# Spectral weights loaded into buffers that attention has finished with, and x put in channel order before its product

## The chip, the cores and the metric

The kernel runs on one core of one Trainium2 chip. The metric is the device time of one execution, in microseconds (us), median of several. A run is called slow when it is over 1.5% above the fastest of the same kernel; only fast runs are compared. The times of single instructions come from the profile of one execution; its span is about 1.8 us shorter than the reported time. In it PE is the engine of the matrix products, DVE, ACT and POOL are the vector, scalar and general engines, and L115 is line 115 of the kernel. POOL also issues the loads, which the DMA engines carry from HBM into SBUF, the memory on the chip; "the queue" is the stream of these loads.

## The reference, cut to what matters

```python
# attention: q, k, v [8, 8, 576, 64], causal window of 64
scores = where(mask, q @ k.T / 8, -1e9);  attn = softmax(scores);  x = attn @ v   # x: [8, 576, 512]
# spectral mix: 64 modes, each with a real and an imaginary 512 x 512 matrix
X = rfft(x, axis=1)[:, :64]
Y = X @ (w_r + 1j * w_i)            # one complex matrix for each mode
y = irfft(Y, n=576, axis=1)
u = x + y
out = u + relu(u @ w_ch)            # w_ch: 512 x 512, "the channel matrix"
```

There are 128 weight matrices (w_r and w_i of 64 modes). Each is 1 MB in HBM as float32 (1.049 million bytes) and becomes 0.524 million bytes in SBUF as bfloat16. They are most of the data that the kernel moves.

## The kernel before: the parts that matter

Attention runs first, in 36 windows of 512 columns. While it runs, POOL issues loads for the first 18 weights, as many as there are buffers (5 in `wlate`, 13 in `wearly`). Then come the modes, each with the two products of its weights. From mode 10 on, one "channel" tile is mixed in after each mode: x times the channel matrix, kept as Z0. The time ends with a tail that turns the spectrum back and writes the result.

```python
    LW, EW = 5, 13
    wlate  = ... tile_pool(name="wlate", bufs=LW)                  # kept through the modes
    wearly = p1 ... tile_pool(name="wearly", bufs=EW, side="right")  # p1: freed after attention
    acons  = p1 ...   # kT, vt of even and odd batches, masks
    rawp   = p1 ... bufs=2       # raw k, q, v of a batch (rk, rq, rv)
    ...
    small  = p1 ... bufs=2       # rcp: reciprocals of the row sums
    ...
    def load_w(i, pool, tag):
        m, im = divmod(i, 2)
        wt = pool.tile([128, NC, DM], BF16, name="wt", tag=tag)
        nc.gpsimd.dma_start(out=wt, in_=src[m].rearrange("(p c) e -> p c e", c=NC))
        wtiles[i] = wt
    ...                                                    # attention, 36 windows
    early(EARLY);  p1.close()
    Z0  = late.tile([128, len(tiles), DM], FP32R, name="Z0")       # over the attention buffers
    wcx = late.tile([128, NC, DM], FP32R, name="wcx", tag="wch")
    nc.gpsimd.dma_start(out=wcx, in_=moe_w_ch.rearrange("(p c) e -> p c e", p=128))

    def mode(m):
        for i in (2 * m, 2 * m + 1):
            if i >= nw:
                load_w(i, wlate, "wl")     # waits until mode has freed one of the five buffers
        ...                                # 32 products psy <- XQ, wt

    def channel(i):
        ... transposes of x_sb[:n, bb, tt, c, :] into pst;  xT = copy of pst
        ... psz = xT @ wcx;  nc.scalar.copy(out=Z0[:, i, :], in_=psz)
        xc = xtp.tile(...)                 # then put x in channel order for the tail
        nc.scalar.copy(out=xc[:n], in_=x_sb[:n, bb, tt, :, :])
        nc.vector.tensor_copy(out=view(x_sb[:n], ...), in_=view(xc[:n], ...))

    for m in range(10 + len(tiles)):
        mode(m)
        if m >= 10: channel(m - 10)
    ...
    wch = late.tile(..., tag="wch")        # the channel matrix again, rows in another order
    nc.gpsimd.dma_start(out=wch, in_=moe_w_ch.rearrange("(c p) e -> p c e", p=128))
    ...                                    # last modes, spectrum, tail
```

PE's order inside attention is fixed by the program (but for a few transposes of the channel stage that stand before its last weighing). On the other engines, and after attention, the compiler's scheduler orders the instructions by their data and their memory. And a tile placed over memory that another tile used waits until that tile is no longer used.

The softmax here doesn't subtract the row's maximum and nothing guards it: scores larger than these inputs give would overflow.

Of the kernel before, what the change touches and what calls it, by code (L numbers as in the profile page):

```python
# [10 lines left out]
FP32R = mybir.dt.float32r  # L11
BF16 = mybir.dt.bfloat16
# [8 lines left out]
def view(ap, off, dims):  # L21

    return bass.AP(ap.tensor, ap.offset + off, [list(ap.ap[0])] + [list(d) for d in dims])
# [3 lines left out]
def kernel(  # L27
# [10 lines left out]
    nc = tc.nc  # L38
    B, H, S, D = q.shape
    NM = moe_w_r.shape[0]  # L40
    DM = moe_w_ch.shape[0]
# [32 lines left out]

    p1 = ExitStack()
    wearly = p1.enter_context(tc.tile_pool(name="wearly", bufs=EW, side="right"))
    acons = p1.enter_context(tc.tile_pool(name="acons", bufs=1, side="right"))
    rawp = p1.enter_context(tc.tile_pool(name="rawp", bufs=2, side="right"))
    qtp = p1.enter_context(tc.tile_pool(name="qtp", bufs=2, side="right"))
    etp = p1.enter_context(tc.tile_pool(name="etp", bufs=4, side="right"))  # L80
    small = p1.enter_context(tc.tile_pool(name="small", bufs=2, side="right"))
# [26 lines left out]

    wtiles = {}

    def load_w(i, pool, tag):
        m, im = divmod(i, 2)
        wt = pool.tile([128, NC, DM], BF16, name="wt", tag=tag)
        src = moe_w_i if im else moe_w_r
        nc.gpsimd.dma_start(out=wt, in_=src[m].rearrange("(p c) e -> p c e", c=NC))  # L115
        wtiles[i] = wt
# [63 lines left out]

    load(1)

    kTs = [acons.tile([128, 4, S], BF16, name=f"kT{i}") for i in range(2)]

    vts = [acons.tile([128, 2, 4, 9, 4, 17], BF16, name=f"vt{i}") for i in range(2)]
    for vt in vts:
        nc.vector.memset(vt[:, 0, :, :, :, 16:17], 1.0)
    pso = ps_o.tile([128, 2, 512], FP32, name="pso")
# [133 lines left out]
    def early(n):  # L322
        nonlocal nw
        for _ in range(n):
            if nw < EARLY:
                load_w(nw, wlate if nw < LW else wearly, "wl" if nw < LW else "we")
                nw += 1

    def warm_up(n):
        for _ in range(n):  # L330
            nc.tensor.matmul(out=pss[2], lhsT=warm[:, 0:128], rhs=warm, start=True, stop=True)
# [3 lines left out]
    with tc.manual_schedule(engines={mybir.EngineType.PE}):  # L335
        warm_up(14)
        first = transpose_units(0)
        for i, j in enumerate((1, 2, 4, 5, 7, 8, 0, 3, 6, 9)):
            first[j]()
            if i in (2, 5):  # L340
                warm_up(6)
            if i in (6, 7, 8):
                warm_up(3)
        load(2)
        early(2)
        NU = 10
        sched = {}

        for b in range(1, B):
            start = -(-9 * (b - 1) // 2)  # L350
            for j in range(NU):
                sched.setdefault(start + j // 3, []).append((b, j))
        units = {}
        mask(0, 1)

        def unit(b, j):
            if b not in units:
                units[b] = transpose_units(b)
            units[b][j]()
            if j == NU - 1:  # L360
                if b + 2 < B:
                    load(b + 2)
                early(3)

        for w in range(NWIN + 1):
            todo = [lambda b=b: dft(b) for b in dfts]
            dfts.clear()
            todo += [lambda b=b, j=j: unit(b, j) for b, j in sched.get(w, [])]
            n = len(todo)
            if w < NWIN:  # L370
                scores(w)
            if w:
                cut = closes(w - 1)
                weigh(w - 1, 8 * w - 8, cut)
            if todo:
                todo.pop(0)()
            if w + 1 < NWIN:
                mask(w + 1, max(1, 3 - n))
            if todo:
                todo.pop(0)()  # L380
            if w:
                weigh(w - 1, cut, 8 * w)
            while todo:
                todo.pop(0)()
        while dfts:
            dft(dfts.pop(0))
        early(EARLY)
# [11 lines left out]
        tiles += [(b + i, t) for i in range(2) for t in range(NT - 1)] + [(b, NT - 1)]  # L399
    p2 = ctx.enter_context(ExitStack())  # L400
    late = p2.enter_context(tc.tile_pool(name="late", bufs=1, side="right", reuse_waits="tile"))
    Z0 = late.tile([128, len(tiles), DM], FP32R, name="Z0")

    trigI = late.tile([128, S + 128], FP32R, name="trigI")

    wcx = late.tile([128, NC, DM], FP32R, name="wcx", tag="wch")
    nc.gpsimd.dma_start(out=wcx, in_=moe_w_ch.rearrange("(p c) e -> p c e", p=128))
    YT = late.tile([128, NC, B, E0], FP32R, name="YT")
    YTl = late.tile([128, NC, 128], FP32R, name="YTl")

    ps_a = p2.enter_context(tc.tile_pool(name="ps_a", bufs=1, space=PSUM, reuse_waits="tile"))
    p2b = ExitStack()
    ps_y = p2b.enter_context(tc.tile_pool(name="ps_y", bufs=2, space=PSUM, reuse_waits="tile"))
    psy = None

    def mode(m):
        nonlocal psy
        for i in (2 * m, 2 * m + 1):
            if i >= nw:
                load_w(i, wlate, "wl")  # L420
        wr, wi = wtiles.pop(2 * m), wtiles.pop(2 * m + 1)
        if m % MG == 0:
            psy = ps_y.tile([128, MG, NC, 2 * B], FP32, name="psy")
        for e in range(NC):
            ee = slice(128 * e, 128 * e + 128)
            for c in range(NC):
                nc.tensor.matmul(out=psy[:, m % MG, e, :], lhsT=wr[:, c, ee],  # L427
                                 rhs=XQ[:, c, :, 1:3, m], start=(c == 0), stop=False)
            for c in range(NC):
                nc.tensor.matmul(out=psy[:, m % MG, e, :], lhsT=wi[:, c, ee],  # L430
                                 rhs=XQ[:, c, :, 0:2, m], start=False, stop=(c == NC - 1))
        if m == NM - 1:
            nc.vector.tensor_copy(
                out=view(YTl, 0, [[128, NC], [MG, 2 * B], [1, MG]]),
                in_=view(psy, 0, [[2 * B, NC], [1, 2 * B], [NC * 2 * B, MG]]))
        elif m % MG == MG - 1:
            for ri in range(2):
                evac(view(YT, m // MG * 2 * MG + ri * MG, [[B * E0, NC], [E0, B], [1, MG]]),
                     view(psy, ri, [[2 * B, NC], [2, B], [NC * 2 * B, MG]]), ri)

    with ExitStack() as p2a:
        ps_t = p2a.enter_context(tc.tile_pool(name="ps_t", bufs=2, space=PSUM, reuse_waits="tile"))
        ps_z = p2a.enter_context(tc.tile_pool(name="ps_z", bufs=2, space=PSUM, reuse_waits="tile"))
        xtp = p2a.enter_context(tc.tile_pool(name="xtp", bufs=2, side="right", reuse_waits="tile"))

        def channel(i):
            b, t = tiles[i]
            pst = ps_t.tile([128, NC, 128], BF16, name="pxt")
            parts = [(b, t, 0, 128)] if t < NT - 1 else [(b, t, 0, 64), (b + 1, t, 64, 64)]
            for bb, tt, r0, n in parts:  # L450
                for c in range(NC):
                    nc.tensor.transpose(out=pst[:, c, r0:r0 + n], in_=x_sb[:n, bb, tt, c, :],  # L452
                                        identity=ident_bf[:n, :n])
            xT = xtp.tile([128, NC, 128], FP32R, name="xT")
            nc.vector.tensor_copy(out=xT, in_=pst)  # L455
            psz = ps_z.tile([128, DM], FP32, name="psz")
            for c in range(NC):
                nc.tensor.matmul(out=psz, lhsT=xT[:, c, :], rhs=wcx[:, c, :],  # L458
                                 start=(c == 0), stop=(c == NC - 1))
            nc.scalar.copy(out=Z0[:, i, :], in_=psz)  # L460

            for bb, tt, r0, n in parts:
                xc = xtp.tile([128, NC, 128], BF16, name="xc")
                nc.scalar.copy(out=xc[:n], in_=x_sb[:n, bb, tt, :, :])  # L464
                nc.vector.tensor_copy(out=view(x_sb[:n], (bb * NT + tt) * DM, [[NC, 128], [1, NC]]),  # L465
                                      in_=view(xc[:n], 0, [[1, 128], [128, NC]]))

        Z_M = 10
        for m in range(Z_M + len(tiles)):
            mode(m)  # L470
            if m >= Z_M:
                channel(m - Z_M)
            if m == 12:

                with tc.tile_pool(name="tmpi", bufs=1, side="right", reuse_waits="tile") as tmp:
                    pcol = tmp.tile([128, 1], FP32, name="pcol")
                    nc.gpsimd.iota(pcol, pattern=[[0, 1]], base=0, channel_multiplier=1,
                                   allow_small_or_imprecise_dtypes=True)
# [38 lines left out]
                                            in0=view(trigI, 0, [[64, 2], [1, 64]]), scalar1=0.0,  # L517
                                            scalar2=None, op0=ALU.mult)

    wch = late.tile([128, NC, DM], FP32R, name="wch", tag="wch")  # L520
    nc.gpsimd.dma_start(out=wch, in_=moe_w_ch.rearrange("(c p) e -> p c e", p=128))
    yap = p2.enter_context(tc.tile_pool(name="yap", bufs=1, side="right", reuse_waits="tile"))

    Yall = yap.tile([128, B, 2, DM], FP32R, name="Yall")
# [22 lines left out]
    with ExitStack() as p3:  # L547
# [11 lines left out]
        for i, (b, t) in enumerate(tiles):  # L559
# [2 lines left out]
            parts = [(b, 0, 128)] if not pair else [(b, 0, 64), (b + 1, 64, 64)]  # L562
            psc = ps_c.tile([128, DM], FP32, name="psc")
            psu = ps_u.tile([128, DM], FP32, name="psu")
            nc.tensor.matmul(out=psc, lhsT=ident_r, rhs=Z0[:, i, :], start=True, stop=False)  # L565
            if fold:
                for bb, r0, n in parts:
                    nc.tensor.matmul(out=psu[r0:r0 + n, :], lhsT=ident_bf[:n, :n],
# [48 lines left out]
```

## Time and profile before

| | before |
|---|---|
| time, median (range), first 3 runs | 481.56 us (481.31 to 482.19) |
| profiled span | 479.5 us |
| last weight lands | 432.2 us |
| DMA queue moves almost nothing | 118.5 to 152.4 us |

The page of the profile cuts the span into 40 slices of 12 us. DMA is the busy share of the DMA engines in tenths, GB/s what they moved, counted as it is written.

```profile
PEclk9899999999995588999987555555555558955999
DMA  9999999999003999999999999999999999993687
GB/s 142 206 208 209 208 212 208 209 213 175 3 3 58 257 214 211 214 214 212 213 214 214 214 213 213 213 213 214 256 213 209 214 214 214 213 182 44 225 302 263
```

The queue is full everywhere but in slices 10 to 12 (120 to 156 us) and in the tail. The next lines are busy times of each engine in two stretches; the last three columns are granted PE clock, DMA share and GB/s.

```profile
core 0: us, PE busy (x) PEld busy (x) DVE busy (x) ACT busy (x) POOL busy (x), PEclk, DMA share, GB/s
180.00:330.00 150.00, 82.66 (x1211) 60.63 (x1211) 40.17 (x76) 37.91 (x68) 33.22 (x62) 0.72 1.06 213
112.00:152.00 40.00, 36.38 (x625) 22.74 (x624) 25.73 (x58) 20.97 (x40) 1.64 (x5) 0.90 0.18 34
```

In the mode stage PE is busy 55% and no other engine more, at 213 GB/s into SBUF. So a weight costs 0.524 MB / 213 GB/s = 2.46 us. Between 112 and 152 us the queue moved 34 GB/s, so 40 x (1 - 34/213) = 33.6 us of it went unused. The groups of instructions say the same (busy us, mean ns, then idle us before them and what ended it): PE waits for weights, and POOL waits for PE to free a buffer.

```profile
L430 PE MATMUL psy<-XQ,wt 128*128 128x16 bf16 x1024 | 62.7, 191 | 84.3 <-DMA wt<-in_moe_w_i_dram 84.1
L427 PE MATMUL psy<-XQ,wt 128*128 128x16 bf16 x1024 | 65.4, 191 | 51.4 <-DMA wt<-in_moe_w_r_dram 49.0
L115 POOL DMA_DIRECT2D wt<-in_moe_w_i_dram x64 | 34.6, 541 | 216.3 <-PE psy L430 197.1
```

The Trainium skill, "Perfetto Trace Analysis", section on what "DMA-bound" means, tells apart a limit in the DMA engines and one in the issuing engine, whose track would be solid with issues. Here an issue takes 0.54 us on POOL and one is needed each 2.46 us, and POOL was busy 33 of 150 us, while the share of the DMA engines was 1.06: it is not the issuing engine but the moving of the data. The timeline of POOL (start, duration, what) shows the hole: the 18th weight is issued at 106.8 us, the 19th at 150.7 us.

```profile
106.80 0.59 POOL L115 DMA_DIRECT2D wt<-in_moe_w_i_dram  x1 [2.06 <-DMA wt<-in_moe_w_r_dram]
140.77 0.14 POOL L477 IOTA pcol<- 128x1 f32 x1 [33.38 <-PE pss_180 L269]
...
150.74 0.54 POOL L115 DMA_DIRECT2D wt<-in_moe_w_r_dram  x1 [9.59 <-PE psy L430]
```

Two more readings serve for comparison. First, the x copies (by tile; min/median/max ns, first and last start): they run from 126 to 256 us.

```profile
L464 ACT COPY xc<-x_sb x40: 612/619/652, 126.1 to 252.5; 128x512 bf16<-128x512 bf16 x32, 64x512 bf16<-64x512 bf16 x8
L465 DVE COPY x_sb<-xc x40: 580/596/618, 143.0 to 256.0; 128x512 bf16<-128x512 bf16 x32, 64x512 bf16<-64x512 bf16 x8
```

The first psx group (the Fourier product of batch 0) and the last pso group (the last weighing of attention). From the start of the first to the end of the last are 142.57 + 0.60 - 40.45 = 102.7 us; this serves as the length of attention.

```profile
40.45 2.02 PE L313 MATMUL psx<-trigF,x_sb 128*128 128x128 bf16 x20
...
142.57 0.60 PE L293 MATMUL pso<-vt_173,et 64*64 64x68 bf16 x18 [0.45 <-DVE x_sb L301]
```

### The profile page before, as it was taken

To read this page: it belongs to the slowest core of one execution; us is meant where nothing else is said; L and a number is where in the kernel's file an instruction comes from. 1 tells how busy PE (TensorE), PEld (TensorE's weight loads), DVE (VectorE), ACT (ScalarE), POOL (GpSimd) and SP (SyncE) were. 2 spreads that over 40 slices of the span, in tenths; PEclk is the share of its full clock that TensorE was granted. 3 is DMA by queue.
4 is the path that set the end of the run, shared out by engine and by line. 5 is a ranking of instruction groups with operands and counts; after the bars stand their busy time and mean duration, and the time that the engine had idled before them with its cause. 6 is when DMAs were issued, how large, how long until landed. Compare 5 with 4: busy or idle time off the path is not lost.

```text
span 479.5 us, 11189 instructions
## 1 busy us (share of the span) xinstructions
PE 319.2 (67%) x4915; PEld 216.7 (45%) x4915; DVE 175.7 (37%) x328; ACT 156.6 (33%) x285; POOL 133.2 (28%) x218
## 2 busy tenths in 40 slices
PE   6999999999988497887877232222132228625995
PEld 3456655665557365655554121222121226413763
DVE  4476767767654046545532000000000002101674
ACT  4565656656633044454532000000000002101663
POOL 8531443240002212211212122122122121200785
PEclk9899999999995588999987555555555558955999
DMA  9999999999003999999999999999999999993687
GB/s 142 206 208 209 208 212 208 209 213 175 3 3 58 257 214 211 214 214 212 213 214 214 214 213 213 213 213 214 256 213 209 214 214 214 213 182 44 225 302 263
DMA packets 38736, 94.04 MB, mean 196 GB/s; under 512 B 3616, under 2 KB 12832, under 8 KB 38560
## 3 DMA queue, kind: packets, MB, share of 16 engines
q0 software_dynamic: 33184, 83.37, 89.1%
q1 hardware_dynamic: 5376, 9.70, 5.9%
q8 instruction: 38, 0.62, 0.5%
q10 hardware_dynamic: 128, 0.26, 0.4%
q14 instruction: 10, 0.08, 0.0%
HBM read 164.63 MB, written 9.44 MB: 363 GB/s over the span
## 4 chain that ended last, share of the span: by engine, by line
DMA 43%; PE 31%; issue 16%; POOL 5%; ACT 4%; DVE 0%; POOLq 0%; DVEq 0%; SPq 0%; ACTq 0%
DMA wt<-in_moe_w_r_dram 28%; DMA wt<-in_moe_w_i_dram 12%; PE pso L293 5%; PE pst L212 3%; PE psx L313 3%; POOL wt L115 2%; PE pss_180 L251 2%; PE psc L574 2%; PE psu L574 2%; DMA rv<-in_v_dram 2%; PE pss_179 L251 2%; PE psc L565 2%; PE pss_178 L251 2%; ACT et L275 1%; ACT qT L58 1%
## 5 line engine op out<-in xcount | busy, mean ns | idle before, releaser
L430 PE MATMUL psy<-XQ,wt 128*128 128x16 bf16 x1024 | 62.7, 191 | 84.3 <-DMA wt<-in_moe_w_i_dram 84.1
L427 PE MATMUL psy<-XQ,wt 128*128 128x16 bf16 x1024 | 65.4, 191 | 51.4 <-DMA wt<-in_moe_w_r_dram 49.0
L115 POOL DMA_DIRECT2D wt<-in_moe_w_i_dram x64 | 34.6, 541 | 216.3 <-PE psy L430 197.1
L430 PEld LDWEIGHTS <-wt 128*128 128x128 bf16 x1024 | 48.5, 104 | 93.5 <-DMA wt<-in_moe_w_i_dram 92.8
L427 PEld LDWEIGHTS <-wt 128*128 128x128 bf16 x1024 | 48.9, 105 | 62.7 <-DMA wt<-in_moe_w_r_dram 58.8
L59 DVE CAST YT<-psy 128x256 fp32r<-128x256 f32 x7 | 3.0, 425 | 141.4 <-PE psy L430 141.3
L458 PE MATMUL psz<-wcx,xT 128*128 128x512 f32 x144 | 48.5, 464 | 3.5 <-DVE xT L455 2.1
L58 ACT CAST YT<-psy 128x256 fp32r<-128x256 f32 x7 | 2.6, 373 | 139.8 <-DVE YT L59 139.8
L455 DVE CAST xT<-pxt 128x512 fp32r<-128x512 bf16 x36 | 24.7, 685 | 45.0 <-PE pxt L452 32.7
L115 POOL DMA_DIRECT2D wt<-in_moe_w_r_dram x64 | 35.0, 546 | 18.9 <-PE psy L430 9.6
L460 ACT CAST Z_3133<-psz 128x512 fp32r<-128x512 f32 x36 | 21.1, 586 | 42.7 <-PE psz L458 42.7
L584 POOL TENSOR_TENSOR ot<-ot,r 128x512 f32<-128x512 f32 x20 | 25.3, 1288 | 24.7 <-DVE ot L582 23.7
L458 PEld LDWEIGHTS psz<-wcx,xT 128*128 128x128 f32 x144 | 28.3, 218 | 8.3 <-issue 2.3
L464 ACT COPY xc<-x_sb 128x512 bf16<-128x512 bf16 (+1 forms) x40 | 24.6, 621 | 19.8 <-DVE x_sb L465 19.8
L293 PEld LDWEIGHTS <-et 128*64 128x64 bf16 (+1 forms) x576 | 22.4, 109 | 14.7 <-issue 7.6
L301 DVE TENSOR_TENSOR x_sb<-pso,rcp 128x640 bf16<-128x640 f32 x32 | 26.4, 824 | 1.0
L465 DVE COPY x_sb<-xc 128x512 bf16<-128x512 bf16 (+1 forms) x40 | 23.7, 596 | 7.7 <-PE pxt L452 7.7
L577 ACT ACTIVATE r<-psc 128x512 f32<-128x512 f32 x36 | 20.9, 598 | 16.0 <-PE psc L574 9.2
L100 POOL DMA_DIRECT2D rv<-in_v_dram x32 | 20.7, 652 | 10.8 <-PE psv_342 L227 3.6
L574 PE MATMUL psc<-Yall,trigI 128*128 128x512 f32 x40 | 18.1, 468 | 4.4 <-DMA Yall<-Yl 4.4
L300 DVE RECIPROCAL rcp<-pso 128x40 f32<-128x40 f32 x32 | 13.0, 405 | 19.3 <-PE pso L293 19.3
L275 ACT ACTIVATE et<-pss_179 128x512 bf16<-128x512 f32 x24 | 14.4, 598 | 9.5 <-PE pss_180 L269 9.5
(244 smaller groups left out, 578.4 us busy)
## 6 DMA issues: line engine op xcount, KB each, us to landing
wt<-in_moe_w_r_dram POOLq DMA_DIRECT2D x64, 512.0 KB, 10.6
wt<-in_moe_w_i_dram POOLq DMA_DIRECT2D x64, 512.0 KB, 8.6
out_dram<-ot SPq DMA_DIRECT2D x32, 256.0 KB, 2.3
rk<-in_k_dram POOLq DMA_DIRECT2D x8, 576.0 KB, 11.5
rq<-in_q_dram POOLq DMA_DIRECT2D x8, 576.0 KB, 11.2
rv<-in_v_dram POOLq DMA_DIRECT2D x32, 144.0 KB, 10.3
wcx<-in_moe_w_ch_dram POOLq DMA_DIRECT2D x1, 1024.0 KB, 11.7
wch<-in_moe_w_ch_dram POOLq DMA_DIRECT2D x1, 1024.0 KB, 10.7
```

The costliest lines, as they stand in the source:

```text
L115: nc.gpsimd.dma_start(out=wt, in_=src[m].rearrange("(p c) e -> p c e", c=NC))
L251: nc.tensor.matmul(out=pss[(2 * w + hh) % 3], lhsT=ident_bf, rhs=view(band, 0, [[0, WIN // 128], [1, 128]]), start=True, stop=False, skip_ ...
L293: nc.tensor.matmul(out=pso[po, hh, (i // 2) * VW:(i // 2 + 1) * VW], lhsT=et[pk, hh, col:col + 64], rhs=vt[pk, 1 - f % 2, 2 * hh + g // 2, ...
L301: nc.vector.tensor_tensor(out=view(x_sb, b * NT * DM + g * 16, [[64, 2], [128, NT * 4], [1, 16]]), in0=view(pso, 0, [[512, 2], [17, NT * 4 ...
L427: nc.tensor.matmul(out=psy[:, m % MG, e, :], lhsT=wr[:, c, ee], rhs=XQ[:, c, :, 1:3, m], start=(c == 0), stop=False)
L430: nc.tensor.matmul(out=psy[:, m % MG, e, :], lhsT=wi[:, c, ee], rhs=XQ[:, c, :, 0:2, m], start=False, stop=(c == NC - 1))
L455: nc.vector.tensor_copy(out=xT, in_=pst)
L458: nc.tensor.matmul(out=psz, lhsT=xT[:, c, :], rhs=wcx[:, c, :], start=(c == 0), stop=(c == NC - 1))
L464: nc.scalar.copy(out=xc[:n], in_=x_sb[:n, bb, tt, :, :])
L465: nc.vector.tensor_copy(out=view(x_sb[:n], (bb * NT + tt) * DM, [[NC, 128], [1, NC]]), in_=view(xc[:n], 0, [[1, 128], [128, NC]]))
L574: nc.tensor.matmul(out=ps, lhsT=trigI[:, tr:tr + 128], rhs=Yall[:, bb, y, :], start=(y == 0 and not fold), stop=(r0 + n == 128))
L584: nc.gpsimd.tensor_tensor(out=ot, in0=ot, in1=r, op=ALU.add)
```

## The change

The intent is to fill the dry stretch. Nine more weights are loaded during attention, into raw k, q, v of the last two batches and into kT and vt of batch 6. Eight more go into a pool `wmid` over the region that attention gives back. x is put in channel order before its product instead of after it, so one copy of the channel matrix serves both uses.

```diff
+    aeven = p1 ... tile_pool(name="aeven", bufs=1, side="right")   # under Z0, not under wmid
...
+    def spare(t):
+        load_w(nw, None, None, view(t, 0, [[DM, NC], [1, DM]]));  nw += 1
+    def spare_raw():
+        spare(rawp.tile(..., name="rk")); spare(rawp.tile(..., name="rq")); spare(rawp.tile(..., name="rv"))
... in unit(b, j), when batch b has been transposed:
+                if b >= B - 2:
+                    early(EARLY)
+                    spare_raw()
... in the window loop:
+            if w == -(-9 * (B - 1) // 2):            # window 32: batch 6 is done
+                spare(kTs[i])
+                for j in range(2):
+                    spare(vts[i][:, j])
... after attention:
-    wcx = late.tile(...); nc.gpsimd.dma_start(out=wcx, in_=moe_w_ch.rearrange("(p c) e -> p c e", p=128))
+    wmid = ... tile_pool(name="wmid", bufs=8, side="right", reuse_waits="tile")
+    MID = nw + 8
+    while nw < MID: load_w(nw, wmid, "wm"); nw += 1
... in mode(m): the loads move behind the products
-        for i in (2 * m, 2 * m + 1):
-            if i >= nw: load_w(i, wlate, "wl")
+        while nw < 2 * NM and (nw - MID if nw < MID + LW else nw - LW) <= 2 * m + 1:
+            load_w(nw, wlate, "wl"); nw += 1
... in channel(i): the two copies of x move ahead of the transposes
+                nc.scalar.copy(out=xc[:n], in_=x_sb[:n, bb, tt, :, :])
+                nc.vector.tensor_copy(out=view(x_sb[:n], ...), in_=view(xc[:n], ...))
                 ... transposes, xT, psz, Z0
-                nc.scalar.copy(out=xc[:n], ...); nc.vector.tensor_copy(out=view(x_sb[:n], ...), ...)
... channels start at mode 15 instead of 10; the matrix is loaded once, after mode 6:
+            if m == 6: nc.gpsimd.dma_start(out=wch, in_=moe_w_ch.rearrange("(c p) e -> p c e", p=128))
-    wch = late.tile(..., tag="wch"); nc.gpsimd.dma_start(out=wch, ...)        # the second copy
```

(Cut: Z0 is split into 34 tiles and 2 later ones, the scratch pools change sides.)

More of the change, by code (lines that the diff above doesn't have):

```diff
@@ L76 @@
     wearly = p1.enter_context(tc.tile_pool(name="wearly", bufs=EW, side="right"))
+    aeven = p1.enter_context(tc.tile_pool(name="aeven", bufs=1, side="right"))
+    rawp = p1.enter_context(tc.tile_pool(name="rawp", bufs=2, side="right"))
     acons = p1.enter_context(tc.tile_pool(name="acons", bufs=1, side="right"))
-    rawp = p1.enter_context(tc.tile_pool(name="rawp", bufs=2, side="right"))
     qtp = p1.enter_context(tc.tile_pool(name="qtp", bufs=2, side="right"))
@@ L109, with load_w @@
     wtiles = {}
-    def load_w(i, pool, tag):
+    def load_w(i, pool, tag, wt=None):
         m, im = divmod(i, 2)
-        wt = pool.tile([128, NC, DM], BF16, name="wt", tag=tag)
+        if wt is None:
+            wt = pool.tile([128, NC, DM], BF16, name="wt", tag=tag)
         src = moe_w_i if im else moe_w_r
@@ L181 @@
     load(1)
-    kTs = [acons.tile([128, 4, S], BF16, name=f"kT{i}") for i in range(2)]
-    vts = [acons.tile([128, 2, 4, 9, 4, 17], BF16, name=f"vt{i}") for i in range(2)]
+    kTs = [p.tile([128, 4, S], BF16, name=f"kT{i}") for i, p in enumerate((aeven, acons))]
+    vts = [p.tile([128, 2, 4, 9, 4, 17], BF16, name=f"vt{i}") for i, p in enumerate((aeven, acons))]
     for vt in vts:
@@ L327, in early @@
                 nw += 1
+    def spare(t):
+        nonlocal nw
+        load_w(nw, None, None, view(t, 0, [[DM, NC], [1, DM]]))
+        nw += 1
+    def spare_raw():
+        spare(rawp.tile([128, 2, RUN * D], BF16, name="rk"))
+        spare(rawp.tile([128, 2, RUN * D], BF16, name="rq"))
+        spare(rawp.tile([128, 9, 4, D], BF16, name="rv"))
     def warm_up(n):
@@ L384 @@
                 todo.pop(0)()
+            if w == -(-9 * (B - 1) // 2):
+                i = (B - 2) % 2
+                spare(kTs[i])
+                for j in range(2):
+                    spare(vts[i][:, j])
         while dfts:
@@ L401 @@
     late = p2.enter_context(tc.tile_pool(name="late", bufs=1, side="right", reuse_waits="tile"))
-    Z0 = late.tile([128, len(tiles), DM], FP32R, name="Z0")
-    trigI = late.tile([128, S + 128], FP32R, name="trigI")
-    wcx = late.tile([128, NC, DM], FP32R, name="wcx", tag="wch")
-    nc.gpsimd.dma_start(out=wcx, in_=moe_w_ch.rearrange("(p c) e -> p c e", p=128))
     YT = late.tile([128, NC, B, E0], FP32R, name="YT")
     YTl = late.tile([128, NC, 128], FP32R, name="YTl")
+    trigI = late.tile([128, S + 128], FP32R, name="trigI")
+    wch = late.tile([128, NC, DM], FP32R, name="wch")
+    ZA = 34
+    Z0a = late.tile([128, ZA, DM], FP32R, name="Z0a")
     ps_a = p2.enter_context(tc.tile_pool(name="ps_a", bufs=1, space=PSUM, reuse_waits="tile"))
+    wm = ExitStack()
+    MW = 8
+    wmid = wm.enter_context(tc.tile_pool(name="wmid", bufs=MW, side="right", reuse_waits="tile"))
+    MID = nw + MW
+    while nw < MID:
+        load_w(nw, wmid, "wm")
+        nw += 1
     p2b = ExitStack()
@@ L416, in mode @@
     def mode(m):
-        nonlocal psy
-        for i in (2 * m, 2 * m + 1):
-            if i >= nw:
-                load_w(i, wlate, "wl")
+        nonlocal psy, nw
         wr, wi = wtiles.pop(2 * m), wtiles.pop(2 * m + 1)
@@ L431, in mode @@
                                  rhs=XQ[:, c, :, 0:2, m], start=False, stop=(c == NC - 1))
+        while nw < 2 * NM and (nw - MID if nw < MID + LW else nw - LW) <= 2 * m + 1:
+            load_w(nw, wlate, "wl")
+            nw += 1
         if m == NM - 1:
@@ L443, with channel_out @@
         ps_z = p2a.enter_context(tc.tile_pool(name="ps_z", bufs=2, space=PSUM, reuse_waits="tile"))
-        xtp = p2a.enter_context(tc.tile_pool(name="xtp", bufs=2, side="right", reuse_waits="tile"))
+        xtp = p2a.enter_context(tc.tile_pool(name="xtp", bufs=2, reuse_waits="tile"))
+        def channel_out(i):
+            return Z0a[:, i, :] if i < ZA else Z0b[:, i - ZA, :]
         def channel(i):
@@ L450, in channel @@
             for bb, tt, r0, n in parts:
+                xc = xtp.tile([128, NC, 128], BF16, name="xc")
+                nc.scalar.copy(out=xc[:n], in_=x_sb[:n, bb, tt, :, :])
+                nc.vector.tensor_copy(out=view(x_sb[:n], (bb * NT + tt) * DM, [[NC, 128], [1, NC]]),
+                                      in_=view(xc[:n], 0, [[1, 128], [128, NC]]))
                 for c in range(NC):
@@ L457, in channel @@
             for c in range(NC):
-                nc.tensor.matmul(out=psz, lhsT=xT[:, c, :], rhs=wcx[:, c, :],
+                nc.tensor.matmul(out=psz, lhsT=xT[:, c, :], rhs=wch[:, c, :],
                                  start=(c == 0), stop=(c == NC - 1))
-            nc.scalar.copy(out=Z0[:, i, :], in_=psz)
-            for bb, tt, r0, n in parts:
-                xc = xtp.tile([128, NC, 128], BF16, name="xc")
-                nc.scalar.copy(out=xc[:n], in_=x_sb[:n, bb, tt, :, :])
-                nc.vector.tensor_copy(out=view(x_sb[:n], (bb * NT + tt) * DM, [[NC, 128], [1, NC]]),
-                                      in_=view(xc[:n], 0, [[1, 128], [128, NC]]))
-        Z_M = 10
+            nc.scalar.copy(out=channel_out(i), in_=psz)
+        Z_M = 15
         for m in range(Z_M + len(tiles)):
             mode(m)
+            if m == 6:
+                nc.gpsimd.dma_start(out=wch, in_=moe_w_ch.rearrange("(c p) e -> p c e", p=128))
+            if m == (MID + 1) // 2:
+                wm.close()
+                zb = p2.enter_context(tc.tile_pool(name="zb", bufs=1, side="right", reuse_waits="tile"))
+                Z0b = zb.tile([128, len(tiles) - ZA, DM], FP32R, name="Z0b")
             if m >= Z_M:
                 channel(m - Z_M)
-            if m == 12:
-                with tc.tile_pool(name="tmpi", bufs=1, side="right", reuse_waits="tile") as tmp:
+            if m == (MID + 1) // 2 + 2:
+                with tc.tile_pool(name="tmpi", bufs=1, reuse_waits="tile") as tmp:
                     pcol = tmp.tile([128, 1], FP32, name="pcol")
@@ L518 @@
                                             scalar2=None, op0=ALU.mult)
-    wch = late.tile([128, NC, DM], FP32R, name="wch", tag="wch")
-    nc.gpsimd.dma_start(out=wch, in_=moe_w_ch.rearrange("(c p) e -> p c e", p=128))
     yap = p2.enter_context(tc.tile_pool(name="yap", bufs=1, side="right", reuse_waits="tile"))
@@ L564 @@
             psu = ps_u.tile([128, DM], FP32, name="psu")
-            nc.tensor.matmul(out=psc, lhsT=ident_r, rhs=Z0[:, i, :], start=True, stop=False)
+            nc.tensor.matmul(out=psc, lhsT=ident_r, rhs=channel_out(i), start=True, stop=False)
             if fold:
```

## The prediction

> **What bounds the kernel now.** From about 152 to 432 us, the DMA queue. The busy table by windows shows a DMA share of 1.06 and 213 GB/s written from 180 to 330 us, while PE is busy 55%, DVE and ACT about 27%. A weight is 1 MB read and 0.524 MB written: 0.524/213 = 2.46 us (estimate from those numbers). The Trainium skill, "DMA: Bandwidth & Descriptors", on the anatomy of one DMA, gives bytes/436e9 for the moving part, 2.41 us for 1 MB; the trace agrees. In the groups of instructions psy waits 84 + 49 us for weights. 18 weights come in during attention; the last two are issued at 104 and 107 us (timeline of POOL), then the buffers are full and the queue is dry from 118.5 to 152.4 us: the next weight is issued at 150.7, when mode 0 has freed a buffer. In the DMA stage 110 weights and two channel matrices (about 2.6 us each: the window with the second moved 255 GB/s) make 276 us, which is the stage. After the last weight lands (432.2 us) comes a tail of 47 us, untouched.
>
> **What the change does.**
> 1. Nine more weights go into buffers that attention has finished with: three when batch 6 has been transposed (about 111 us), three for batch 7 (125), three in kT and vt of batch 6 (131). 9 x 2.46 = 22 us moves into the dry stretch, all on the critical path.
> 2. Eight follow into the region that attention gives back, as soon as its last weighing is done (143 us, the first perhaps at 140.5), not at 150.7. Of the dry 34 us, 12 remain after point 1; I expect 8 to 10 of them gained.
> 3. One channel matrix instead of two: -2.6 us of queue.
> 4. Reordering x first only moves an ACT copy (0.62 us) and a DVE copy (0.60 us) per tile ahead of the transposes, on engines with 70% free: 0.
> 5. A possible new gap: weight 40 may only be issued after mode 17, and the channel matrix lands behind 13 weights, at about 179 us. If PE's order puts products of channels 0 and 1 before mode 17, the queue idles 5 to 8 us around 182 to 189. If mode 17 comes first (its weights land near 168), there is none. I give the gap 30%.
>
> Sum: from 118.5 us, 110 weights + one matrix = 273 us, so 391.5; plus 2 to 4 us of small gaps, plus 4.5 us from the end of the full-rate stream to the last landing as before: last weight at 398 to 400, against 432.2. Gain 32 to 34 us; with the gap of point 5, 25 to 28. Attention's pace does not suffer: two batches took 31.0 us with the queue dry and 31.1 with it full (starts of the psx groups).
>
> **Predicted: 449 us, 8 in 10 between 443.5 and 456.** Faster by over 2%: 0.97; within 2%: 0.02; slower: 0.01.
>
> **What would show each step.** DMA row: 9s through slices 10 to 12. POOL timeline: weight issues near 111, 125, 131 and 140 to 147 us. Stage rate still 213 GB/s. Last psy near 399 us, tail still 47 us. Point 5: a dip of the DMA row near 182 to 189 us, the first psz waiting on the channel matrix.
>
> **What would make it wrong.** A long gap at weight 40; spare loads issued late because POOL waits in order; channel products bunching and stalling modes; attention slowed by the loads.

## The result

| | before | after |
|---|---|---|
| time, median of 4 runs | 481.44 us (481.19 to 482.19) | 452.95 us (451.99 to 454.00) |
| profiled span | 479.5 us | 450.2 us |
| last weight lands | 432.2 us | 403.4 us |
| queue unused between 112 and 152 us | 33.6 us | 8.5 us |

The ratio of after to before is 0.9406, 95% interval 0.9381 to 0.9432. Ratios are the mean time of one kernel's fast runs over that of the other's of the same rounds, so they are not quite the ratios of the medians quoted.

The same lines of the page, after:

```profile
PEclk9999999999999655596996997555555559555999
DMA  8999999999995899999999999999999999973787
GB/s 140 205 209 208 211 209 209 211 208 208 214 197 115 168 214 213 260 212 214 214 213 213 214 214 213 214 214 214 213 213 214 205 213 214 213 142 48 280 298 262
```

A slice is now 11.3 us. The two slices without traffic are gone; a dip is left in slices 12 and 13 (135 to 158 us). The same stretches:

```profile
180.00:330.00 150.00, 90.34 (x1251) 66.86 (x1251) 31.51 (x72) 25.30 (x47) 31.88 (x63) 0.74 1.07 217
112.00:152.00 40.00, 36.23 (x637) 22.51 (x631) 29.77 (x54) 25.37 (x49) 9.12 (x16) 0.96 0.88 168
```

Of the 40 us, 40 x (1 - 168/213) = 8.5 us are unused. The rate in the mode stage is as before (the 217 holds the one channel matrix, which stays float32 in SBUF and so writes twice the bytes of a weight). In the same 40 us DVE and ACT have become busier, by 4.0 and 4.4 us. PE still waits for weights, less:

```profile
L457 PE MATMUL psy<-XQ,wt 128*128 128x16 bf16 x960 | 58.9, 191 | 62.5 <-DMA wt<-in_moe_w_i_dram 62.3
L454 PE MATMUL psy<-XQ,wt 128*128 128x16 bf16 x944 | 60.2, 191 | 44.7 <-DMA wt<-in_moe_w_r_dram 37.4
L118 POOL DMA_DIRECT2D wt<-in_moe_w_i_dram x60 | 33.5, 559 | 191.6 <-PE psy L457 148.4
```

(The counts are lower because these loads and products now carry other tile names: rk, kT and so on.) The timeline of POOL, some of its issues:

```profile
109.41 0.53 POOL L118 DMA_DIRECT2D rk<-in_moe_w_r_dram  x1 [1.95 <-PE psv_2406 L230]
...
121.19 0.53 POOL L118 DMA_DIRECT2D rk<-in_moe_w_i_dram  x1 [7.66 <-PE pst L215]
...
129.34 0.53 POOL L118 DMA_DIRECT2D kT_173<-in_moe_w_r_dram  x1 [1.54 <-PE pso L296]
...
132.95 0.54 POOL L118 DMA_DIRECT2D vt_175<-in_moe_w_i_dram  x1
146.77 0.53 POOL L118 DMA_DIRECT2D wt<-in_moe_w_i_dram  x1 [13.29 <-DVE x_sb L304]
...
176.37 0.53 POOL L118 DMA_DIRECT2D wt<-in_moe_w_r_dram  x1 [9.94 <-PE psy L457]
```

The nine spare loads came about when forecast. The first load into the returned region came at 146.8 us, later than forecast, and what it waited for is DVE's last normalisation of x (line 304), not PE's last weighing. The last line is weight 40, released by mode 17: the queue was then still busy with the channel matrix (it moved 297 GB/s between 180 and 186 us), so no gap opened there.

The x copies and attention:

```profile
L487 ACT COPY xc<-x_sb x40: 612/618/637, 37.3 to 151.1; 128x512 bf16<-128x512 bf16 x32, 64x512 bf16<-64x512 bf16 x8
L488 DVE COPY x_sb<-xc x40: 584/600/626, 40.9 to 151.7; 128x512 bf16<-128x512 bf16 x32, 64x512 bf16<-64x512 bf16 x8
```

```profile
39.12 2.02 PE L316 MATMUL psx<-trigF,x_sb 128*128 128x128 bf16 x20
...
143.84 0.60 PE L296 MATMUL pso<-vt_176,et 64*64 64x68 bf16 x18 [0.16 <-DVE x_sb L304]
```

This was not foreseen. No copy is left in the stage it was written for: all 80 now start between 37 and 152 us. The copies no longer wait for the product, so the scheduler placed them as soon as a batch of x was complete, most of them into attention. And attention takes 143.84 + 0.60 - 39.12 = 105.3 us instead of 102.7. Two batches of attention now take 32.1 us (psx groups at 71.22 and 103.32 us) where they took 31.1 (71.55 and 102.65).

### The profile page after: what moved, and what is told of

It reads as the page before. It is cut to its first block, busy times and chain, and to the rows that moved or that the text cites. A ratio compares the mean times of both kernels' runs of the same rounds, so it can differ in the third digit from the quotient of the medians.

```text
span 450.2 us, 11163 instructions
## 1 busy us (share of the span) xinstructions
PE 315.7 (70%) x4915; PEld 215.0 (48%) x4915; DVE 175.0 (39%) x328; ACT 153.9 (34%) x285; POOL 133.2 (30%) x217
## 5 line engine op out<-in xcount | busy, mean ns | idle before, releaser
L457 PE MATMUL psy<-XQ,wt 128*128 128x16 bf16 x960 | 58.9, 191 | 62.5 <-DMA wt<-in_moe_w_i_dram 62.3
L454 PE MATMUL psy<-XQ,wt 128*128 128x16 bf16 x944 | 60.2, 191 | 44.7 <-DMA wt<-in_moe_w_r_dram 37.4
L118 POOL DMA_DIRECT2D wt<-in_moe_w_i_dram x60 | 33.5, 559 | 191.6 <-PE psy L457 148.4
L457 PEld LDWEIGHTS <-wt 128*128 128x128 bf16 x960 | 45.7, 104 | 70.4 <-DMA wt<-in_moe_w_i_dram 69.8
L454 PEld LDWEIGHTS <-wt 128*128 128x128 bf16 x944 | 45.1, 104 | 55.6 <-DMA wt<-in_moe_w_r_dram 46.9
L497 PE MATMUL psz<-wch,xT 128*128 128x512 f32 x144 | 48.2, 465 | 2.8 <-DMA wch<-in_moe_w_ch_dram 1.7
L494 DVE CAST xT<-pxt 128x512 fp32r<-128x512 bf16 x36 | 23.7, 686 | 62.2 <-PE pxt L491 46.5
L499 ACT CAST Z0a<-psz 128x512 fp32r<-128x512 f32 x34 | 19.8, 586 | 68.9 <-PE psz L497 54.6
L118 POOL DMA_DIRECT2D wt<-in_moe_w_r_dram x59 | 31.9, 541 | 23.1 <-PE psy L457 9.9
L497 PEld LDWEIGHTS psz<-wch,xT 128*128 128x128 f32 x144 | 28.5, 218 | 8.1 <-DMA wch<-in_moe_w_ch_dram 1.8
L487 ACT COPY xc<-x_sb 128x512 bf16<-128x512 bf16 (+1 forms) x40 | 23.9, 619 | 14.2 <-DVE x_sb L488 7.9
```

The lines of the kernel that those rows point to most:

```text
L454: nc.tensor.matmul(out=psy[:, m % MG, e, :], lhsT=wr[:, c, ee], rhs=XQ[:, c, :, 1:3, m], start=(c == 0), stop=False)
L457: nc.tensor.matmul(out=psy[:, m % MG, e, :], lhsT=wi[:, c, ee], rhs=XQ[:, c, :, 0:2, m], start=False, stop=(c == NC - 1))
L494: nc.vector.tensor_copy(out=xT, in_=pst)
L497: nc.tensor.matmul(out=psz, lhsT=xT[:, c, :], rhs=wch[:, c, :], start=(c == 0), stop=(c == NC - 1))
```

## The experiments

Eleven kernels were run, in three calls; the runs of one call share a chip and its runs of the kernel before. "After" means the changed kernel. Where kernels of different calls are compared, the ratio to before is used.

| run | change to after | median us (range) | ratio to before | attention us | first load into region |
|---|---|---|---|---|---|
| e0_after | none | 452.73 (452.10 to 454.18) | 0.9407 | 105.4 | 146.9 |
| e1_no_spares | nine spare loads out | 476.15 (475.20 to 476.76) | 0.9882 | 105.3 | 148.5 |
| e2_no_mid | eight early loads out | 464.15 (460.57 to 478.11) | 0.9609 | 105.3 | 159.7 |
| e4_x_late | x copies after attention | 450.79 (450.45 to 451.17) | 0.9357 | 103.3 | 144.6 |
| e3_two_matrices | second channel matrix | 456.72 (454.84 to 457.08) | 0.9460 | 105.3 | 148.4 |
| e5_small_apart | reciprocals elsewhere | 452.38 (451.25 to 456.37) | 0.9410 | 105.3 | 145.2 |
| e6_apart_x_late | e4 and e5 | 449.90 (449.19 to 456.71) | 0.9325 | 102.3 | 143.6 |
| e8_fill | e6, two more weights | 446.19 (445.35 to 447.52) | 0.9258 | 103.7 | 143.5 |
| e9_keep_warm | 4 warming products | 452.79 (452.34 to 453.11) | 0.9397 | 105.3 | 146.8 |
| e10_no_mid_warm | e2 and e9 | 459.70 (458.75 to 461.85) | 0.9549 | 105.3 | 152.3 |
| e11_fill_warm | e8 and e9 | 448.17 (447.14 to 448.51) | 0.9301 | 103.6 | 143.7 |

Without the early loads (e2, e10) the last column is the load that mode 0 releases. "Attention" is from the first psx group to the end of the last weighing. One run of e2 (478.11 us) and one of e6 (456.71 us) were slow: medians and ranges are of all runs, the ratios of fast runs alone. All outputs were correct.

### What the nine spare loads are worth, and whether their traffic slows attention

> Control: the kernel after again, on the chip of the other runs of this call. Both theories: within 1 us of 453 us; attention's last weighing ends near 144.4 us, the first load into the returned region is issued near 146.8 us, the queue is dry from about 141.5 to 148.2 us.

The control gave what was expected: 452.73 us, and the first load into the returned region at 146.9 us.

```diff
-                    spare_raw()
-                spare(kTs[i])
-                for j in range(2):
-                    spare(vts[i][:, j])
```

> The nine loads into finished attention buffers are taken out, all else stays. Theory (queue-bound: each weight moved into the dry stretch saves its own transfer of 2.46 us): 9 x 2.46 = 22 us slower than the kernel after, about 475 us. Rival (part of the nine only shifts a wait that something else hides): clearly less, 5 to 15 us. Also: if attention's later end (144.4 instead of 143.2 us) comes from the added DMA traffic, it goes back to 143.2 here; if it comes from the x copies that the schedule pulls into attention, it stays near 144.4.

It is 23.4 us slower than the control. In its profile the first psx group stands at 40.78 us against 39.18 in the control's, so up to 1.6 us of that is a late start (see below) and about 22 us the nine weights, as the queue's arithmetic says. Attention takes 105.4 us with these loads (the control) and 105.3 without them (145.52 + 0.60 - 40.78): their traffic does not slow it.

```profile
40.78 2.02 PE L316 MATMUL psx<-trigF,x_sb 128*128 128x128 bf16 x20
...
145.52 0.60 PE L296 MATMUL pso<-vt,et 64*64 64x68 bf16 x18 [0.16 <-DVE x_sb L304]
```

### What the eight early loads are worth

```diff
-    MW = 8
-    wmid = wm.enter_context(tc.tile_pool(name="wmid", bufs=MW, side="right", reuse_waits="tile"))
+    MW = 0
```

> The eight loads into the region that attention returns are taken out: after the nine spares, the next load is the one that mode 0 releases. Theory: those eight are worth only the earlier start of the queue (148.2 against about 151.7 us), so 3 to 4 us slower than the kernel after, about 456 us. Rival (each of the eight is worth its own transfer): 8 x 2.46 = 20 us slower, about 473 us.

The result was neither. The fast runs took 460.6, 461.1 and 467.2 us, their middle 8.4 us above the control; by ratio it is (0.9609 - 0.9407) x 481.6 = 9.7 us. The profiled run (467.2 us) has its first psx group at 48.0 us, 8.8 us late, before anything that the edit touches. So this run mixes two things and had to be repeated (e10 below).

### The spread between runs

The same lines of three profiles show what the late start is: the stretch from 20 to 24 us in e0 (first psx group at 39.2 us), e3 (40.7 us) and e2 (48.0 us). The figure after the comma is PE's busy time, the third column from the end the granted clock.

```profile
20.00:24.00 4.00, 3.58 (x84) 2.15 (x74) 2.60 (x4) 3.76 (x7) 3.18 (x6) 1.00 1.21 210
```

```profile
20.00:24.00 4.00, 3.30 (x37) 1.77 (x37) 1.18 (x3) 2.56 (x5) 2.73 (x5) 0.72 1.22 210
```

```profile
20.00:24.00 4.00, 3.47 (x30) 1.68 (x32) 0.50 (x2) 1.65 (x5) 2.51 (x5) 0.59 1.23 211
```

Near 19 us PE waits for the values of batch 1. Its idle time there summed to 0.4 us in e0, 1.0 us in e3 and 1.4 us in e2; the clock stayed at 1.00, fell to 0.50 for about 3 us, and fell to 0.50 for about 24 us. In e2 the two waits (in brackets) are these, at the start of the stretch shown and just before it:

```profile
20.12 0.30 PE L230 MATMUL psv<-rv,pick 32*128 32x320 bf16 x1 [0.95 <-DMA rv<-in_v_dram]
20.84 1.24 PE L230 MATMUL psv<-rv,pick 32*128 32x320 bf16 x7 [0.41 <-DMA rv<-in_v_dram]
```

The Trainium skill, "TensorE: Matmul & The Clock Gate", Part 1, describes this gate: half clock after an idle window of about 3.4 us, full clock after a busy one. The half and the full clock agree with these traces, the length of the idle does not: all five profiles with 0.97 to 1.4 us of idle there (before, e1, e2, e3, e6) show the fall to 0.50, the eight with 0.46 us or less do not. The test puts four products in front of that gap:

```diff
+            if w == 0:
+                warm_up(4)          # 128x512 products on zeros, before the first unit of batch 1
```

> The kernel after, with four more warming products on PE before it waits for the values of batch 1 (near 19 us). In the traces so far PE idles 0.4 to 1.4 us there; with 0.4 its clock stays at 1.00, with 1.0 it is at 0.50 for 3 us and attention is 1.5 us later, with 1.4 it is at 0.50 for 24 us and attention is 8.8 us later. Theory (this idle gap, a matter of chance, makes the spread between runs of one kernel): first psx group at 39 to 39.5 us, the runs lie within 1 us of one another, median near 452.2 us. Rival (the spread comes from elsewhere): runs still between 452 and 454 us or wider.

The range of the five runs fell from about 2 us to 0.8 us and the clock stayed at 1.00; the median, at 452.8 us, did not fall. So the gap makes the late starts, and on the whole costs this kernel little. That it makes all of the spread is not shown: e4 without the products has a range of 0.7 us, e10 with them one of 3.1 us.

> The kernel without the eight early loads, with the same four products, so that the late clock no longer hides what those loads are worth. Theory: queue dry 4 us longer than in the kernel after, and a little lost after it: 4 to 6.5 us above the warm run of this call, 456 to 459 us. Rival: each early load is worth its own 2.46 us: 20 us above.

It is 6.9 us above e9, a little more than the 4 to 6.5 us expected, so the eight early loads are worth 7 us, not 20 us. The line that carries this, from its timeline of POOL: the first load after the spares comes 5.6 us later than in e9 (146.78 us), when mode 0 has run.

```profile
152.34 0.56 POOL L118 DMA_DIRECT2D wt<-in_moe_w_i_dram  x1 [5.11 <-PE psy L458]
```

The windows of 2 us show the queue dry about 4.6 us longer than in e9; the rest, about 2 us, is lost at reduced rate between 154 and 160 us and between 170 and 176 us. Why the rate is lower there was not tested. (The profiled run is the slowest of the six: its last psy comes 7.9 us after that of e9, and 0.6 us of this is a later first psx.)

### The second channel matrix

```diff
+    nc.gpsimd.dma_start(out=wch, in_=moe_w_ch.rearrange("(c p) e -> p c e", p=128))   # after the channels
```

> The channel matrix is loaded a second time after the channel products, as the kernel before does; all else is the kernel after. Theory: it costs its own queue time, 1 MB read like a weight, 2.5 us more than the kernel after's 452.7 us, about 455.2 us. Rival (the second load hides in the stage): no change, below 0.5 us.

The ratio rises from 0.9407 to 0.9460, which is 0.0053 x 481.7 = 2.6 us. The two intervals touch (0.9383 to 0.9432, 0.9420 to 0.9499), but the profiles agree: the last psy comes at 408.25 us against 404.15 in e0, 4.1 us later, of which 1.5 us is a late start (first psx at 40.71 against 39.18). The median rose more, as three of its five runs had the lower mean clock of about 0.78; the other two, at 0.80, took 454.8 and 454.9 us.

### The copies of x inside attention

The copies are scaled by a one that is computed from the last result of attention. The result is the same number, and none of them can run earlier.

```diff
+        nc.vector.tensor_scalar(out=one, in0=view(x_sb, (B - 1) * NT * DM + 48, [[1, 1]]),
+                                scalar1=0.0, scalar2=1.0, op0=ALU.mult, op1=ALU.add)
-                nc.scalar.copy(out=xc[:n], in_=x_sb[:n, bb, tt, :, :])
+                nc.scalar.activation(out=xc[:n], in_=x_sb[:n, bb, tt, :, :], func=ACT_F.Copy, scale=one[:n])
```

> The copies that put x in channel order are made to depend on the last result of attention (scale by a one computed from it), so that none can run during attention. Theory (these 80 copies on ACT and DVE delay attention): no x copy before 145 us, last weighing ends near 143.2 us instead of 144.4, the first load into the returned region is issued near 145.5 instead of 146.8, and the time falls by 1 to 1.5 us. Rival (DMA traffic delays attention): last weighing still at 144.4 us, time unchanged or worse, as the copies now stand in the way of the first modes.

```profile
L491 ACT ACTIVATE xc<-x_sb,one x40: 706/722/725, 144.2 to 184.7; 128x512 bf16<-128x512 bf16 x32, 64x512 bf16<-64x512 bf16 x8
L493 DVE COPY x_sb<-xc x40: 576/607/631, 145.0 to 185.9; 128x512 bf16<-128x512 bf16 x32, 64x512 bf16<-64x512 bf16 x8
```

```profile
142.04 0.60 PE L297 MATMUL pso<-vt,et 64*64 64x68 bf16 x18 [1.35 <-DVE x_sb L305]
144.57 0.53 POOL L119 DMA_DIRECT2D wt<-in_moe_w_i_dram  x1 [12.80 <-DVE one L478]
```

Attention takes 103.3 us, the first load is issued at 144.6 us, and the time falls by 1.9 us (the intervals of the ratios do not overlap). With e1 this settles it: the copies lengthen attention, the traffic of the nine loads does not. They cost 2.0 to 3.1 us of attention (105.3 against 103.3 here and 102.3 in e6). The two differ by a wait for the values of a later batch (0.7 us for loads between 98 and 118 us) that e6, whose attention began 1.4 us later, does not have: the step between two psx groups takes 14.2 us here (101.53 to 115.75) and 13.2 us there.

### What the first early load waits for

```diff
-    small = p1.enter_context(tc.tile_pool(name="small", bufs=2, side="right"))
+    small = ctx.enter_context(tc.tile_pool(name="small", bufs=2))      # outside the returned region
```

> The small pool (reciprocals of the row sums, 320 bytes) is moved out of the region that the eight early loads take over; the x copies still run during attention. Theory (the first of the eight lies over the reciprocals and so waits for DVE's last normalisation instead of PE's last weighing): the first load is issued within 0.5 us of the end of the last weighing, near 145 us instead of 146.9, and the time falls by about 2 us to 450.7. Rival (POOL waits for something else, or order of issue): still 2.3 us after the last weighing, no change.

The last weighing and the first load in its profile:

```profile
144.02 0.59 PE L296 MATMUL pso<-vt,et 64*64 64x68 bf16 x18 [0.16 <-DVE x_sb L304]
...
145.16 0.53 POOL L118 DMA_DIRECT2D wt<-in_moe_w_i_dram  x1 [11.48 <-issue]
```

The load now follows the end of the last weighing by 0.55 us instead of 2.3 us. The cause of these 1.8 us is shown: 320 bytes of reciprocals lay under the first of the eight buffers. The time itself is inconclusive: two of six runs took 456 us, the other four 451.3 to 453.1 us, and the interval of the ratio (0.9361 to 0.9460) holds no change as well as a gain of 2 us. What made those two runs late was not traced.

> Both: the small pool moved, and the x copies kept out of attention. Theory (the two delays add): from the first psx group to the end of the last weighing 103.3 us instead of 105.3, first load near 143 us, the time about 449 us (3.5 to 4 us below the kernel after). Rival (they overlap): no better than the better one of the two alone, 450.7 us.

Both together give 0.9325, that is (0.9407 - 0.9325) x 481.7 = 3.9 us below after. Attention takes 102.3 us, and the first load comes at 143.6 us, 0.54 us after the last weighing: the profile shows both delays gone. The time fits their sum but does not prove it: e5 alone showed no clear gain, and the interval (0.9284 to 0.9365) reaches into that of e4 (0.9342 to 0.9372).

### Filling what is left

```diff
     (e6, and)
+    qTt = [p.tile([128, 4, S], BF16, name=f"qT{i}") for i, p in enumerate((aeven, acons))]   # replaces qtp
+                spare(qTt[i])                       # with kT and vt of batch 6
+    wextra = ... tile_pool(name="wextra", bufs=1)   # where the trigonometric scratch was; weight 18
-    ZA = 34
+    ZA = len(tiles)                                 # so that all of Z0 lies over the spares
-    MW = 8
+    MW = 6
```

> Both, and two more weights during attention: one in qT of batch 6, one where the scratch of the trigonometric tables was; six instead of eight loads into the returned region. Theory (what is left of the gain is the dry stretch alone): the queue is dry for under 1 us between 118 and 150 us, and the time is 2 x 2.46 us below the run before it, 444 to 445 us. Rival (the stage after it is no longer bound by the queue once the dry stretch is gone, or weight 40 now waits for mode 17): a new gap near 180 us, and the time stays at 447 us or more.

```profile
DMA  8999999999999999999999999999999999954687
GB/s 139 204 210 206 213 210 208 212 208 209 213 213 208 208 213 247 202 199 212 212 212 213 214 213 214 213 213 214 212 213 212 199 214 213 213 120 94 239 304 259
```

The row has no dip left between the start and the tail. The median is 446.19 us, ratio 0.9258 (0.9221 to 0.9295), which lies clear of the interval of after: it beats both kernels. Against e6 the gain is (0.9325 - 0.9258) x 481.7 = 3.2 us where 4.9 us were expected; the time fell between the theory and its rival. The windows of 2 us show a part of the rival, small new shortages behind the matrix: 178 and 195 GB/s from 178 to 182 us and 199, 170 and 190 from 188 to 194. With 162 GB/s from 144 to 146 us these lose, against 213, about 1.7 us (estimate from these rates), which is what is missing.

> The filled queue (both delays removed, two more weights in attention, six early loads) with the same four products. Theory: as e8_fill but without its late runs, 445.3 to 446 us with runs within 1 us of each other. Rival: no change from 446.2 us and the same spread of 2 us.

This missed: 448.2 us, 2 us worse than e8 by ratio (the intervals overlap: 0.9278 to 0.9324, 0.9221 to 0.9295), though its range did shrink to 1.4 us. Its profile shows the same full queue; why the last weight comes 1.5 us later (400.0 against 398.5 us for the last psy) stays open.

## Why the prediction was right, and where its terms were off

The time, 452.95 us, lies in the stated range of 443.5 to 456, and 4 us above the middle.

- *The DMA queue bounds the kernel, 2.46 us for a weight.* Right. The rate after is 212 to 214 GB/s in the slices of the mode stage without the matrix (one has 205), and e1 gives about 22 us for nine weights.
- *Point 1, nine weights, 22 us.* Right: 23.4 us in e1, with up to 1.6 us of late start. The issues came at 109 to 113, 121 to 127 and 129 to 133 us.
- *Point 2, "I expect 8 to 10 of them gained" of the 12 us left.* This is the term that failed in size. The dry time fell from 33.6 to 8.5 us, by 25 us; with 22 from point 1, 3 us are left for the earlier start. The step that failed is "as soon as its last weighing is done (143 us, the first perhaps at 140.5)": the load came at 146.8 us. Attention had become longer (e4), so that the last weighing ended at 144.4 us instead of 143.2, and the load came 2.3 us after it, as the first buffer lay over the reciprocals and waited for DVE (e5: 1.8 us of it).
- *Point 3, one matrix less, 2.6 us.* Right: e3 gives 2.6 us by ratio.
- *Point 4, reordering x first: "0".* Wrong, though small. It assumed that a copy stays in the stage where the text has it, on engines with 70% free. It moved into attention, where DVE has less free time (before, it was busy 25.7 of the 40 us from 112 to 152 us), and made attention 2.0 to 3.1 us longer; taking it out gains 1.9 us (e4).
- *"Attention's pace does not suffer."* Right for what was argued, the traffic (e1: 105.4 us with, 105.3 without), and wrong as a whole, because of point 4. The profile of before began attention 1.3 us later than that of after (first psx at 40.45 and 39.12 us), which hid half of it. The forecast's own evidence was thin: the two batches that it calls dry began at 102.7 us, 16 us before the queue ran dry.
- *Point 5, a gap at weight 40, 30%.* It did not come. Mode 17 was ordered before the channel products, and weight 40 was issued at 176.4 us with the matrix still to be moved. What the other order would have cost was not tested.
- *The sum.* Small gaps were put at 2 to 4 us and measured 8.5 us, which covers the miss of 4 us (with 8.5 us the sum puts the last landing at 404.5 us). The last weight landed at 403.4 us instead of 398 to 400, and the tail was 450.2 - 403.4 = 46.8 us, as forecast.

## What to carry to other kernels

When one queue bounds a kernel, count the time in which it moves nothing, and find which buffer stops it: each load moved into that time is worth its own transfer, while an early start of many loads is worth little more than the dry time that it ends (here 7 us for eight loads, of which 4.6 us were dry). Removing a dependence lets the scheduler move work into another stage, where the engines may have less time free; before calling an operation free, ask where it will run when nothing holds it back. A load into reused memory waits for the last reader of what lay there, so keep small tiles with late readers out of the region that is reused first.

## What the Trainium skill lacked or had wrong

- "TensorE: Matmul & The Clock Gate", Part 1, gives an idle window of about 3.4 us before the clock halves. Here about 1.0 us of idle within 2 us (e3) was followed by a clock of 0.50 for about 3 us, 1.4 us of idle (e2) by 0.50 for about 24 us, though PE was busy all the while (12.00 of the 12 us from 28 to 40 us), and 0.4 us (e0) by none. A later section of the page, on a second failure mode, does say that frequent short idles can make the clock fall, but gives no length.
- "DMA: Bandwidth & Descriptors", section on the anatomy of one DMA: its bytes/436e9 gives, as an estimate, 2.41 us for the moving part of 1 MB and agrees with the 2.46 us of a weight in the full queue. No page was found that says how fast a stream of converting loads comes back to full rate after a dry stretch; after e10's restart the queue ran at 170 to 180 GB/s for 6 us before it reached 213.
- No page tells that removing a dependence can move work into an earlier stage of the program; here it cost attention 2.0 to 3.1 us (e4, e6).
